# Two-part attention probabilities: one transposing transfer of 128 rows for each half tile in place of two of 64, and one planned time for every transposition

## The chip, the cores and the metric

One NeuronCore of a Trainium2 chip runs the whole program in one launch. The metric is device time in microseconds (us); several executions of a kernel are timed and their median is given. Engines are TensorE (PE, with its weight loads PEld), VectorE (DVE), ScalarE (ACT), GpSimd (POOL) and SyncE (SP), which here only issues transfers. Each engine works through its own instructions in the order in which the program lists them; semaphores order them across engines.

## The reference

```python
# q, k, v: (8 batches, 8 heads, 576 positions, 64), float32
scores = (1 / sqrt(64)) * q @ k.transpose(0, 1, 3, 2)
mask = (rel >= 0) & (rel < 64)            # rel = query position - key position
attn = softmax(where(mask, scores, -1e9))
x = (attn @ v).transpose(0, 2, 1, 3).reshape(8, 576, 512)
mixed = real(fft(fft(x, axis=1), axis=2))
u = x + mixed
un = (u - mean(u)) / sqrt(var(u) + 1e-06)     # over the last axis
out = u + maximum(un @ w_ch1, 0) @ w_ch2      # 512 -> 2048 -> 512
```

## The kernel before

The 8 x 576 rows of tokens are 36 tiles of 128 (`T` = 0 to 35, function `attn_tile`). Each pair of batches (nine tiles) then goes through a two-dimensional Fourier transform (`fft`), each tile through the normalization (`norm_tile`), and each pair of tiles is one *chunk* of 256 tokens of the feed-forward part (`ffn`, 18 chunks, 16 hidden blocks `f` each). In `ffn`, `ph` (L1213) is the first matrix product, `hh` its relu in two float16 parts (ACT L1228 writes the high part, DVE L1231 the low part), and `po` (L1194) the second product. The first chunk is computed in float32 (`PLAIN`), the others from float16 pairs, a high and a low part, in three passes (`PASSES`).

The attention of tiles 0 to 12 is in float32 (`whole`); its transpositions are done on PE. From tile 13 (`PRO`) on it is in two parts, and the transpositions are done by transfers that SP issues: `k_turn` (L493, into `kst`), two `q_turn` (L505, into `qbd`), and `p_turn` (L632, into `pt`). A tile has two half tiles (`jj` = 0, 1) of 64 queries and 8 heads. For one of them `score` (L581) leaves on each of 128 partitions (head parity x 64 queries) four head pairs x 128 keys; `masked` (L593, DVE) applies the mask and finds the maximum, `expo` (L601, ACT) the exponential, `p_hi` and `p_lo` (L403 and L413, or L407 where DVE does it) split it into the two parts in a buffer `flex[:, 1 + jj]`, seen as `pp` [128, 4, 2, 128] float16. `p_turn(0)` and `p_turn(1)` then transpose 64 rows of `pp` each into `pt` [128 keys, 2, 4, 2 x 64]. `av` (L663, PE) multiplies `pt` by the values `va`, `ve`, for both half tiles together, and `normed` (L671 to L675, DVE) divides by the sums. `y_turn` (L771, into `py`) and, in `norm_tile`, `u_turn` (L1056, into `uhl`, the input of a chunk) are transposing transfers too, of 128 rows x 1024 columns, as `k_turn` is.

The order of the instructions on every engine is made by a list scheduler, `Plan`, when the program is built. Each piece of work is an `op(engine, duration, priority, function, reads, writes, lat, alt)`. A transfer occupies the planner's engine "DMA" (SP's queue) for its duration, and what depends on it is thought ready `lat` later. `alt` names a second engine that may take the piece where it would be done sooner. `slack` adds half a microsecond before PE work that depends on a transfer (from tile 9 on). The numbers decide the order and the choice of engine only; on the chip semaphores decide. The lines of the transpositions before:

```python
TURN = 1.26
HTURN = 1.2
op("DMA", TURN, base + 0.2, k_turn, [bkp], [bkT], lat=2.0)
op("DMA", TURN, base + 0.7, lambda j=j: q_turn(j), Bfl[4:6], [Bq[i]], lat=2.8)
op("DMA", HTURN, base + 4.2 + jj, lambda g=p_turn: g(0), [bpp], [bt, bt2], lat=1.8)
op("DMA", HTURN, base + 4.3 + jj, lambda g=p_turn: g(1), [bpp], [bt2], lat=1.8)
op("DMA", TURN, base + 7.7, y_turn, [byp], [bpy], lat=2.2)
op("DMA", TURN, base + 0.95, u_turn, [bup, Bwl] if c >= 2 else [bup], [bu], lat=2.2)
```

The feed-forward products have the lowest priority (1e6 and up), so that PE takes them wherever no attention or Fourier work is ready.

Of the kernel before, what the change touches and what calls it, by code (L numbers as in the profile page):

```python
# [27 lines left out]
P = 128  # L28
# [8 lines left out]
NCH = NTT // 2  # L37
NKF = DFF // P
XR = 10
TURN = 1.26  # L40
HTURN = 1.2
Y_SOON = (4, 8)
LAZY, LAZY_FFT, LAZY_U = 0.2, 0.8, 0.5
LAZY_E, LAZY_Y = 0.3, 0.8
# [253 lines left out]
def attn_fft_ffn_kernel(ctx: ExitStack, tc: tile.TileContext, q, k, v, w1, w2, gidx, dft_d, dft_s, mask, out):  # L298
# [17 lines left out]
    def sb(shape, dt, tag, name):  # L316
        return pl.tile(shape, dt, tag=tag, name=name, bufs=RINGS[tag])
# [99 lines left out]
    def attn_tile(T, base):  # L417
# [145 lines left out]
        for jj in range(2):  # L563
# [61 lines left out]
                pp = t["pp", jj]  # L625
                both(eng, pp[:, :, 1], t["pr", jj], pp[:, :, 0], ALU.subtract)

            def p_turn(h, jj=jj):
                if h == 0:
                    t["pt", jj] = sb([P, 2, 4, P], F16, "pt", f"pt{T}_{jj}")  # L630
                dst = t["pt", jj][:, h].rearrange("p a (z s) -> p (a z) s", z=2)
                nc.sync.dma_start_transpose(dst, t["pp", jj][64 * h : 64 * h + 64].rearrange("p a z t -> p (a z t)"))  # L632

            op("ACT", 0.52, base + 4 + jj, p_hi, [bp], [bpp], alt=("DVE", 0.34, lazy))
            op("POOL", 1.12, base + 4.1 + jj, p_lo, [bp], [bpp], alt=("DVE", 0.6, lazy))
            bt2 = Buf()
            bpt[jj] = [bt, bt2]
            op("DMA", HTURN, base + 4.2 + jj, lambda g=p_turn: g(0), [bpp], [bt, bt2], lat=1.8)
            op("DMA", HTURN, base + 4.3 + jj, lambda g=p_turn: g(1), [bpp], [bt2], lat=1.8)

        bx, by = Buf("xu"), Buf("y")
        Bx[T] = bx
# [2 lines left out]
        for hf in range(2):  # L645
            bpa = Buf("ps")

            def av(hf=hf):
                if hf == 0:
                    xts[T] = sb([P, DM], F32, "xu", f"xu{T}")  # L650
                pa = t["pa", hf] = bank("ps", f"pa{T}_{hf}", (P, 4, 65))
                for hh in range(4):
                    h = 4 * hf + hh
                    if whole:
                        mm = [(slice(64 * (h % 2), 64 * (h % 2) + 64), None)]
                    else:
                        mm = [(slice(64 * a, 64 * a + 64), b_) for a, b_ in PASSES]

                    for x, (sl, b_) in enumerate(mm):
                        for jj, vt in enumerate(vts):  # L660
                            pt = t["pt", jj][:, h // 2] if whole else t["pt", jj][:, h % 2, h // 2]
                            v_ = vt[:, h] if whole else vt[:, b_, h]
                            nc.tensor.matmul(  # L663
                                pa[64 * jj : 64 * jj + 64, hh], pt[:, sl], v_, start=(x == 0), stop=(x == len(mm) - 1)
                            )
# [658 lines left out]
```

## Time and profile before

| what | value |
|---|---|
| median of 3 runs (lowest to highest) | 1008.24 us (1006.14 to 1009.97) |
| profiled execution | 1003.44 us, of it the span 1001.5 us |
| PE busy | 967.4 us (97%) |
| PE weight loads busy | 685.3 us (68%) |
| DVE busy | 665.6 us (66%) |
| ACT busy | 418.2 us (42%) |
| POOL busy | 260.9 us (26%) |
| chain that ended last, by engine | PE 80%, DMA 8%, SP 3%, DVE 3% |
| mean granted clock of TensorE | 0.996 |

The span runs from the first to the last instruction; the run's time is some 2 us longer. A profiled execution is one of many, here 4.8 us below the median of the timed ones.

### The profile page before, as it was taken

What the parts mean: (1) busy time and instruction counts of PE and PEld (TensorE: products, weight loads), DVE (VectorE), ACT (ScalarE), POOL (GpSimd) and SP (SyncE); (2) the same over time, 40 slices, a digit from 0 to 9 for tenths busy, and PEclk for the clock granted to TensorE, in tenths of its full rate; (3) what the DMA queues carried; (4) which work ended last, traced back from release to release, by engine and by line L of the source; (5) the groups of instructions that cost most, each with busy time, mean ns of one, the idle gap of its engine ahead of it and who ended that gap; (6) DMA issues with size and microseconds to landing.
All of it is one profiled execution on the core that took longest, in us unless ns stands there. A gap on an engine that the chain in (4) does not pass through costs nothing.

```text
span 1001.5 us, 22810 instructions
## 1 busy us (share of the span) xinstructions
PE 967.4 (97%) x8756; PEld 685.3 (68%) x8756; DVE 665.6 (66%) x1979; ACT 418.2 (42%) x1047; POOL 260.9 (26%) x537
## 2 busy tenths in 40 slices
PE   7889989999999989999999999999999999999998
PEld 6677757677776757676676667766676667666664
DVE  5899989888786768565796758676686745432121
ACT  6666656844554436323354426333454212121111
POOL 1000110136364623453032405343022400320000
PEclk9999999999999999999999999999999999999999
DMA  8987684225889877867768766968566311230000
GB/s 191 251 218 210 174 194 121 79 57 114 148 167 166 169 114 148 154 142 144 137 115 176 139 125 108 190 127 152 97 103 125 85 33 46 53 75 22 1 22 22
DMA packets 310540, 123.08 MB, mean 123 GB/s; under 512 B 292568, under 2 KB 292696, under 8 KB 310432
## 3 DMA queue, kind: packets, MB, share of 16 engines
q1 hardware_dynamic: 307712, 112.71, 55.4%
q0 software_dynamic: 2720, 8.92, 3.2%
q8 instruction: 69, 1.13, 0.5%
q14 instruction: 39, 0.32, 0.1%
HBM read 54.97 MB, written 14.17 MB: 69 GB/s over the span
## 4 chain that ended last, share of the span: by engine, by line
PE 80%; DMA 8%; SPq 3%; DVE 3%; issue 2%; ACT 2%; POOL 1%; DVEq 0%; POOLq 0%; ACTq 0%
PE ph L1213 34%; PE po L1194 32%; DMA kn<-in_k 3%; PE pa L663 3%; PE pz L930 2%; PE psc L581 2%; PE pg L896 2%; DMA pt<-flex 2%; PE psc L574 2%; POOL flex L413 1%; SPq L632 1%; DMA kst<-flex 1%; PE pp L612 1%; SPq L505 1%; DMA qn<-in_q 1%
## 5 line engine op out<-in xcount | busy, mean ns | idle before, releaser
L1213 PE MATMUL ph<-uhl,w0s 128*128 128x256 f16 (+1 forms) x3384 | 426.2, 277 | 4.3 <-DVE hh L1231 4.1
L1194 PE MATMUL po<-w1s,hh 128*128 128x512 f16 (+1 forms) x1696 | 426.0, 387 | 0.0
L1213 PEld LDWEIGHTS <-w0s 128*128 128x128 f16 x3264 | 317.7, 98 | 91.2 <-issue 8.0
L1231 DVE SCALAR_TENSOR_TENSOR hh<-ph,hh 128x256 f16<-128x256 f32 x272 | 114.5, 422 | 232.6 <-ACT hh L1228 228.9
L1228 ACT ACTIVATE hh<-ph 128x256 f16<-128x256 f32 x272 | 103.6, 382 | 382.2 <-PE ph L1213 288.2
L1194 PEld LDWEIGHTS <-hh 128*128 128x128 f16 x1632 | 156.5, 98 | 137.5
L601 ACT ACTIVATE pr<-pr,nm 128x128 f32<-128x128 f32 x288 | 90.9, 392 | 11.0 <-DVE nm L593 11.0
L593 DVE CUSTOM_DVE_ANT_0 pr<-psc,mskb 128x128 f32<-128x128 f32 x288 | 65.6, 284 | 15.7 <-PE psc L574 10.9
L413 POOL TENSOR_TENSOR up<-un,up 128x128 f16<-128x128 f32 x132 | 56.0, 452 | 64.8 <-ACT up L403 62.2
L413 POOL TENSOR_TENSOR flex<-kn,flex 128x128 f16<-128x128 f32 x76 | 40.4, 561 | 111.9 <-ACT flex L403 85.3
L413 POOL TENSOR_TENSOR flex<-pr,flex 128x128 f16<-128x128 f32 x92 | 38.7, 451 | 117.4 <-ACT flex L403 88.6
L1028 POOL TENSOR_TENSOR rs<-mv,mhalf 128x1 f32<-128x1 f32 x36 | 21.1, 585 | 139.9 <-DVE mv L1024 133.2
L1004 POOL DMA_INDIRECT mt<-md,gix x34 | 35.9, 1056 | 49.4 <-DMA md<-mp 42.8
L413 POOL TENSOR_TENSOR flex<-qn,flex 128x128 f16<-128x128 f32 x96 | 44.5, 496 | 14.1 <-ACT flex L403 10.9
L663 PE MATMUL pa<-va,pt 128*64 128x65 f16 (+1 forms) x760 | 38.9, 204 | 5.7 <-DMA pt<-flex 5.6
L663 PE MATMUL pa<-ve,pt 128*64 128x65 f16 (+1 forms) x760 | 39.3, 204 | 0.1
L403 ACT CAST flex<-pr 128x512 f16<-128x512 f32 x39 | 24.0, 615 | 24.1 <-DMA pt<-flex 22.9
L675 DVE TENSOR_TENSOR xu<-pa,rc 128x256 f32<-128x256 f32 x72 | 30.5, 424 | 2.6
L574 PE MATMUL psc<-kst,qbd 128*128 128x128 f32 x208 | 28.2, 282 | 3.5 <-ACT pt L403 1.5
L930 PE MATMUL pz<-g,ds__75 97*96 97x257 f16 (+3 forms) x240 | 29.2, 273 | 0.8 <-DVE g L906 0.8
L574 PEld LDWEIGHTS psc<-kst,qbd 128*128 128x128 f32 x208 | 25.1, 192 | 6.2 <-ACT pt L403 2.3
L663 PEld LDWEIGHTS <-pt 128*64 128x64 f16 x1104 | 20.3, 111 | 12.9 <-issue 6.6
(155 smaller groups left out, 1100.9 us busy)
## 6 DMA issues: line engine op xcount, KB each, us to landing
wd<-in_moe_w_ch SPq DMA_DIRECT2D x20, 512.0 KB, 4.7
out<-xu SPq DMA_DIRECT2D x36, 256.0 KB, 2.5
ve<-va SPq DMA_DIRECT2D x67, 130.0 KB, 3.3
kn<-in_k SPq DMA_DIRECT2D x32, 256.0 KB, 3.9
qn<-in_q SPq DMA_DIRECT2D x32, 256.0 KB, 4.7
flex<-in_moe_w_ch SPq DMA_DIRECT2D x12, 512.0 KB, 6.5
flex<-in_v SPq DMA_DIRECT2D x20, 256.0 KB, 3.5
md<-mp SPq DMA_DIRECT2D x24, 192.0 KB, 2.9
```

What stands on the lines that cost most here:

```text
L413: eng.tensor_tensor(out=out[:, k : k + w], in0=in0[:, k : k + w], in1=in1[:, k : k + w], op=al)
L574: nc.tensor.matmul(p_[:, hp], qw, keys(hp, jj), start=True, stop=True)
L593: nc.vector.tensor_tensor_reduce(out=t["pr", jj][:, hp], in0=t["ps", jj][:, hp], in1=mskb[:, m : m + P], scale=-0.125, scalar=3.0e38, op0= ...
L601: nc.scalar.activation(pr, pr, AF.Exp, bias=t["nm", jj][:, hp : hp + 1], scale=-1.0)
L663: nc.tensor.matmul(pa[64 * jj : 64 * jj + 64, hh], pt[:, sl], v_, start=(x == 0), stop=(x == len(mm) - 1))
L675: nc.vector.tensor_tensor(out=xv[:, 4 * hf : 4 * hf + 4], in0=pa[:, :, 0:64], in1=rc.to_broadcast([P, 4, 64]), op=ALU.mult)
L930: nc.tensor.matmul(pz[:M, c0:c1], ds_[:NJ, a, c[0] : c[0] + c[1]], t["g", gi][:, b_, c0:c1], start=(x == 0), stop=(x == len(mm) - 1),)
L1004: nc.gpsimd.indirect_dma_start(out=mts[T], out_offset=None, in_=mds[pb][0 : HR if n < 4 else 2 * HR], in_offset=bass.IndirectOffsetOnAxis( ...
L1194: nc.tensor.matmul(t["po"][i], l_, r_, start=(f == 0 and x == 0), stop=(f == NKF - 1 and x == len(mm) - 1))
L1213: nc.tensor.matmul(ph, l_, r_, start=(x == 0), stop=(x == len(mm) - 1))
L1228: nc.scalar.activation(t["hh", f][:, 0], ph, AF.Relu)
L1231: nc.vector.scalar_tensor_tensor(out=hh[:, 1], in0=ph, scalar=0.0, in1=hh[:, 0], op0=ALU.max, op1=ALU.subtract)
```

## The change

For each half tile of tiles 13 to 35 the two transfers of 64 rows become one of 128 rows, and `pt` is laid out as [128 keys, 4 pairs, 2 parts, 128 rows], from which `av` takes slices of 64 columns as before. The planner's time for this transfer and for the other transpositions (`k_turn`, `q_turn`, `y_turn`, `u_turn`) becomes 1.5, and the `lat` of `p_turn` 2.2. The transfers of k, q, y and u, the pieces into which the work is cut, and all arithmetic stay.

```diff
--- before.py
+++ after.py
@@ -37,8 +37,7 @@
 NCH = NTT // 2
 NKF = DFF // P
 XR = 10
-TURN = 1.26
-HTURN = 1.2
+TURN = 1.5
 Y_SOON = (4, 8)
 LAZY, LAZY_FFT, LAZY_U = 0.2, 0.8, 0.5
 LAZY_E, LAZY_Y = 0.3, 0.8
@@ -625,18 +624,14 @@
                 pp = t["pp", jj]
                 both(eng, pp[:, :, 1], t["pr", jj], pp[:, :, 0], ALU.subtract)
 
-            def p_turn(h, jj=jj):
-                if h == 0:
-                    t["pt", jj] = sb([P, 2, 4, P], F16, "pt", f"pt{T}_{jj}")
-                dst = t["pt", jj][:, h].rearrange("p a (z s) -> p (a z) s", z=2)
-                nc.sync.dma_start_transpose(dst, t["pp", jj][64 * h : 64 * h + 64].rearrange("p a z t -> p (a z t)"))
+            def p_turn(jj=jj):
+                t["pt", jj] = sb([P, 4, 2, P], F16, "pt", f"pt{T}_{jj}")
+                dst = t["pt", jj].rearrange("p a z s -> p (a z) s")
+                nc.sync.dma_start_transpose(dst, t["pp", jj].rearrange("p a z t -> p (a z t)"))
 
             op("ACT", 0.52, base + 4 + jj, p_hi, [bp], [bpp], alt=("DVE", 0.34, lazy))
             op("POOL", 1.12, base + 4.1 + jj, p_lo, [bp], [bpp], alt=("DVE", 0.6, lazy))
-            bt2 = Buf()
-            bpt[jj] = [bt, bt2]
-            op("DMA", HTURN, base + 4.2 + jj, lambda g=p_turn: g(0), [bpp], [bt, bt2], lat=1.8)
-            op("DMA", HTURN, base + 4.3 + jj, lambda g=p_turn: g(1), [bpp], [bt2], lat=1.8)
+            op("DMA", TURN, base + 4.2 + jj, p_turn, [bpp], [bt], lat=2.2)
 
         bx, by = Buf("xu"), Buf("y")
         Bx[T] = bx
@@ -651,14 +646,11 @@
                 pa = t["pa", hf] = bank("ps", f"pa{T}_{hf}", (P, 4, 65))
                 for hh in range(4):
                     h = 4 * hf + hh
-                    if whole:
-                        mm = [(slice(64 * (h % 2), 64 * (h % 2) + 64), None)]
-                    else:
-                        mm = [(slice(64 * a, 64 * a + 64), b_) for a, b_ in PASSES]
-
-                    for x, (sl, b_) in enumerate(mm):
+                    sl = slice(64 * (h % 2), 64 * (h % 2) + 64)
+                    mm = [(None, None)] if whole else PASSES
+                    for x, (a, b_) in enumerate(mm):
                         for jj, vt in enumerate(vts):
-                            pt = t["pt", jj][:, h // 2] if whole else t["pt", jj][:, h % 2, h // 2]
+                            pt = t["pt", jj][:, h // 2] if whole else t["pt", jj][:, h // 2, a]
                             v_ = vt[:, h] if whole else vt[:, b_, h]
                             nc.tensor.matmul(
                                 pa[64 * jj : 64 * jj + 64, hh], pt[:, sl], v_, start=(x == 0), stop=(x == len(mm) - 1)
```

As the planner's numbers change, the order changes on every engine from about 130 us of the program on. Line numbers of the changed kernel are 1 lower ahead of `p_turn` and 8 lower behind `av`. Three places follow; names with a number at their end are buffers.

SP's queue at tile 17 (`pt` of both half tiles, with the turns of k and q around them and a load of k), before:

```order
L632 DMA_TRANSPOSE pt_0_4881<-flex 128x8x64
L505 DMA_TRANSPOSE qbd_77<-flex 128x16x64
L493 DMA_TRANSPOSE kst<-flex 128x8x128
L632 DMA_TRANSPOSE pt_0_4881<-flex 128x8x64
L632 DMA_TRANSPOSE pt_1_4934<-flex 128x8x64
L505 DMA_TRANSPOSE qbd_77<-flex 128x16x64
L433 DMA kn_4964<-in_k 128x8x64
L632 DMA_TRANSPOSE pt_1_4934<-flex 128x8x64
```

The same place of the changed kernel:

```order
L630 DMA_TRANSPOSE pt_0_4882<-flex 128x8x128
L504 DMA_TRANSPOSE qbd_76<-flex 128x16x64
L432 DMA qn_4907<-in_q 128x8x64
L630 DMA_TRANSPOSE pt_1_4919<-flex 128x8x128
L504 DMA_TRANSPOSE qbd_76<-flex 128x16x64
L492 DMA_TRANSPOSE kst<-flex 128x8x128
L432 DMA kn_4987<-in_k 64x8x64 x2
```

The four issues into `pt` (8 x 64) have become two (8 x 128), one for each half tile, and a load of q stands between them.

DVE at the conversion of the last of the first matrix's weights (`wf_15`, three instructions, for which the first chunk's block 12, counted from 0, waits), behind the Fourier work of the second batch (`fs`, `h`), before:

```order
L413 TENSOR_TENSOR fs_1_1839<-f_1_1833,fs_1_1839 128x388
L413 TENSOR_TENSOR fs_1_1857<-f_1_1825,fs_1_1857 128x388
L1105 TENSOR_SCALAR wf_15_1864<-flex 128x512
L1110 SCALAR_TENSOR_TENSOR wf_15_1864<-flex,wf_15_1864 128x512
L1117 SCALAR_TENSOR_TENSOR wf_15_1864<-flex,wf_15_1864 128x512
L413 TENSOR_TENSOR h_1_1868<-yT_805 128x388
L413 TENSOR_TENSOR h_1_1877<-yT_805 128x388
```

The same place of the changed kernel:

```order
L412 TENSOR_TENSOR fs_1_1837<-f_1_1826,fs_1_1837 128x388
L412 TENSOR_TENSOR fs_1_1854<-f_1_1813,fs_1_1854 128x388
L412 TENSOR_TENSOR h_1_1862<-yT_805 128x388
L1097 TENSOR_SCALAR wf_15_1866<-flex 128x512
L1102 SCALAR_TENSOR_TENSOR wf_15_1866<-flex,wf_15_1866 128x512
L1109 SCALAR_TENSOR_TENSOR wf_15_1866<-flex,wf_15_1866 128x512
L412 TENSOR_TENSOR h_1_1872<-yT_805 128x388
```

One of the two additions into `h` has moved ahead of the three instructions on `wf_15`.

DVE between the statistics of tile 4 and those of tile 5 (these two tiles' normalized rows are the input of chunk 2); `un` is the scaled tile 4, `rc` and `xu` are `normed`, `w0s` and `w1s` are splits of weights. Before, behind the statistics of tile 4:

```order
L1231 SCALAR_TENSOR_TENSOR hh_10_2518<-ph_10_2490,hh_10_2518 128x256
L1231 SCALAR_TENSOR_TENSOR hh_11_2542<-ph_10_2490,hh_11_2542 128x256
L671 TENSOR_SCALAR rc_1_2547<-pa_1_2218 128x4
L674 RECIPROCAL rc_1_2547<-rc_1_2547 128x4
L675 TENSOR_TENSOR xu_2371<-pa_1_2218,rc_1_2547 128x256
L1170 SCALAR_TENSOR_TENSOR w1s<-w1s,s_89 128x512
L1032 TENSOR_SCALAR un_2571<-xu_651,mv_2515,rs_2540 128x512
L1231 SCALAR_TENSOR_TENSOR hh_12_2573<-ph_12_2551,hh_12_2573 128x256
L1170 SCALAR_TENSOR_TENSOR w1s<-w1s,s_89 128x512
```

The same place of the changed kernel:

```order
L1223 SCALAR_TENSOR_TENSOR hh_10_2597<-ph_10_2568,hh_10_2597 128x256
L663 TENSOR_SCALAR rc_0_2622<-pa_0_2543 128x4
L666 RECIPROCAL rc_0_2622<-rc_0_2622 128x4
L667 TENSOR_TENSOR xu_2542<-pa_0_2543,rc_0_2622 128x256
L663 TENSOR_SCALAR rc_1_2636<-pa_1_2554 128x4
L666 RECIPROCAL rc_1_2636<-rc_1_2636 128x4
L667 TENSOR_TENSOR xu_2542<-pa_1_2554,rc_1_2636 128x256
L1223 SCALAR_TENSOR_TENSOR hh_11_2634<-ph_10_2568,hh_11_2634 128x256
L1162 SCALAR_TENSOR_TENSOR w0s<-wf_15_1866,s_88,w0s 128x512
L1162 SCALAR_TENSOR_TENSOR w1s<-w1s,s_89 128x512
L1024 TENSOR_SCALAR un_2665<-xu_651,mv_2587,rs_2620 128x512
L1162 SCALAR_TENSOR_TENSOR w1s<-w1s,s_89 128x512
```

Before, one half of `normed` (tile 10) stood here; now two halves (tile 11) and a split into `w0s` stand here, and the scaling into `un` comes behind them. Of the rows not shown that stand ahead of tile 5's statistics, the changed kernel has two more half tiles' `masked` (tile 12), one more cast of weights on DVE (L404, which ACT did before) and one more split of weights (`w1s`); each of the two halves of `normed` of tile 11 came behind these statistics before, and that of tile 10 now stands ahead of tile 4's. On PE the changed kernel has three pieces ahead of chunk 2's first block that came behind it before: `flip_p` of tile 12 (L612), one half of `av` of tile 12 (L663) and `flip_y` of tile 11 (L756).

## Rows read from the trace of the kernel before

**Rows 1.** Busy time in two stretches of the span: the stretch, its length, busy us (and instructions) of PE, PEld, DVE, ACT and POOL, then the granted clock, the busy share of the DMA engines and GB/s.

```profile
200.00:250.00 50.00, 50.00 (x424) 35.04 (x423) 41.96 (x134) 22.83 (x54) 23.25 (x49) 1.00 0.39 86
250.00:800.00 550.00, 539.21 (x5432) 377.18 (x5431) 385.76 (x1164) 230.97 (x580) 199.67 (x412) 1.00 0.74 138
```

**Rows 2.** What PE waited for from 250 to 800 us: us in total, times, the longest.

```profile
PE pa L663 <- DMA pt<-flex: 5.6, 5, 2.1
PE ph L1213 <- DVE hh L1231: 4.1, 5, 1.3
PE py L756 <- DVE y L413: 0.8, 1, 0.8
```

**Rows 3.** PE's instructions behind these waits, in order of time: start, us, instruction, and in brackets PE's idle time before it and what ended it.

```profile
309.09 0.22 PE L663 MATMUL pa<-va,pt 128*64 128x65 f16 x1 [2.10 <-DMA pt<-flex]
362.30 0.22 PE L663 MATMUL pa<-va,pt 128*64 128x65 f16 x1 [1.43 <-DMA pt<-flex]
375.56 0.22 PE L663 MATMUL pa<-va,pt 128*64 128x65 f16 x1 [0.93 <-DMA pt<-flex]
412.54 0.22 PE L663 MATMUL pa<-va,pt 128*64 128x65 f16 x1 [0.73 <-DMA pt<-flex]
735.40 0.22 PE L663 MATMUL pa<-va,pt 128*64 128x65 f16 x1 [0.41 <-DMA pt<-flex]
459.29 0.27 PE L1213 MATMUL ph<-uhl,w0s 128*128 128x256 f16 x1 [1.30 <-DVE hh L1231]
545.37 0.27 PE L1213 MATMUL ph<-uhl,w0s 128*128 128x256 f16 x1 [1.25 <-DVE hh L1231]
```

**Rows 4.** The transposing transfers on SP: ns that the issue of one took (least, median, most) with the first and last start, and under each the us from issue to landing (least, median, most). L632 turns 64 rows, L1056 and L493 128 rows x 1024 columns, L505 64 rows x 2048 columns.

```profile
L632 SPq DMA_TRANSPOSE pt<-flex x92: 1192/1268/2390, 251.7 to 807.9; - x92
...
DMA to landing us min/median/max: 2.6/3.3/4.7
...
L1056 SPq DMA_TRANSPOSE uhl<-up x34: 1231/1241/2144, 122.5 to 893.3; - x34
...
DMA to landing us min/median/max: 3.0/3.4/5.4
...
L493 SPq DMA_TRANSPOSE kst<-flex x23: 1231/1314/3172, 157.0 to 723.9; - x23
...
DMA to landing us min/median/max: 3.3/3.8/4.3
...
L505 SPq DMA_TRANSPOSE qbd<-flex x46: 1242/1326/2503, 230.9 to 735.1; - x46
...
DMA to landing us min/median/max: 3.6/3.8/5.3
```

**Rows 5.** Pieces of the chain of work that ended last, around three of the waits: start, us, what.

```profile
302.03 7.01 DMA pt<-flex
...
309.09 0.85 PE pa L663 x41
...
452.09 4.92 DMA kst<-flex
...
537.70 5.28 DMA qbd<-flex
```

**Rows 6.** DVE, then PE, around the first chunk's wait for weights: start, us, instruction, idle time before it and what ended it.

```profile
144.48 0.43 DVE L1105 TENSOR_SCALAR w0s<-flex 128x512 int32<-128x512 int32 x1 [0.93 <-DMA flex<-in_moe_w_ch]
...
151.07 1.02 DVE L413 TENSOR_TENSOR h<-yT 128x388 f32<-128x388 f32 x2
...
151.23 0.80 PE L1213 MATMUL ph<-uhl,wf 128*128 128x256 f32 x1 [3.96 <-DVE wf L1117]
```

**Rows 7.** Three short stretches, columns as in Rows 1: just behind that wait, just behind the wait of 2.10 us, and DVE's stretch ahead of tile 5's statistics.

```profile
150.90:154.30 3.40, 3.07 (x7) 2.53 (x8) 3.33 (x8) 1.93 (x5) 0.00 (x0) 0.50 0.15 59
...
309.10:312.50 3.40, 3.40 (x60) 2.51 (x61) 2.12 (x8) 1.63 (x3) 1.95 (x5) 1.00 1.29 276
...
202.20:211.95 9.75, 9.75 (x68) 6.46 (x66) 8.03 (x26) 5.01 (x12) 3.20 (x6) 1.00 0.09 28
```

**Rows 8.** Around the start of chunk 2, in order of time on SP (the two turns of its input: start of the first, time to the end of the second), PE (a piece of the chain each for L663, two halves of `av`, and L756, then the timeline) and DVE (a cast; the first and the last of a half tile's four `masked`; a split; the first and the last instruction of two halves of `normed`).

```profile
211.18 7.61 SPq L1056 DMA_TRANSPOSE uhl<-up x2
...
214.84 1.08 PE pa L663 x32
...
221.34 0.44 PE py L756 x4
...
222.91 0.27 PE L1213 MATMUL ph<-uhl,w0s 128*128 128x256 f16 x1
...
195.21 0.49 DVE L405 TENSOR_SCALAR w1s<-w1s,s 128x512 f16<-128x512 f32 x1
...
209.63 0.28 DVE L593 CUSTOM_DVE_ANT_0 pr<-psc,mskb 128x128 f32<-128x128 f32 x1
...
210.26 0.28 DVE L593 CUSTOM_DVE_ANT_0 pr<-psc,mskb 128x128 f32<-128x128 f32 x1
...
211.29 0.74 DVE L1170 SCALAR_TENSOR_TENSOR w1s<-w1s,s 128x512 f16<-128x512 f32 x1
...
215.50 0.16 DVE L671 TENSOR_SCALAR rc<-pa 128x4 f32<-128x4 f32 x1 [0.28 <-PE pa L663]
...
216.65 0.42 DVE L675 TENSOR_TENSOR xu<-pa,rc 128x256 f32<-128x256 f32 x1
```

## The prediction

> **What bounds the kernel now.** I read the busy time by stretches first. From 200 to 250 us PE is never idle, and from 250 to 800 us, where all the two-part attention lies, it is idle for 550 - 539.2 = 10.8 us [rows 1]. So the products' own time sets the end, nothing that this change could do to transfers shortens them, and all that it can win in the stretch it acts on is 10.8 us, 1.1% of the span. The view of waits then says what those 10.8 us are: 5.6 us in five waits for turned probabilities, 4.1 us for relu parts, 0.8 us for a Fourier input [rows 2]. Five waits over 23 tiles: most turns land under feed-forward products and cost PE nothing. The timeline gives their sizes, 2.10, 1.43, 0.93, 0.73 and 0.41 us [rows 3]. The chain shows two more things. The longest wait ends a transfer that took 7.01 us from issue to landing, far over the median; and two of the waits for relu parts begin with other transposing transfers, one into `kst` of 4.92 us and one into `qbd` of 5.28 us [rows 5]: ACT's next piece waits for the buffer they read, and the relu behind it is late for PE.
>
> **The new transfer.** It removes 46 of 92 issues, 1.27 us of SP each [rows 4], some 58 us. SP computes nothing, so this counts only through landings. The trace has no 128-row turn of `pt`, but it has the same shape, 128 rows x 1024 columns, into `uhl` and `kst`: issue 1.24 to 1.31 us, landing 3.4 to 3.8 us after it [rows 4]. Twice the rows cost SP nothing more and the landing 0.1 to 0.5 us; I take 3.6. A pair of 64 rows issued back to back is complete 1.27 + 3.3 = 4.57 us after its first issue, the single one after 3.6: 0.97 us sooner. The planner takes part of this back. It thought the pair ready 1.2 + 1.2 + 1.8 = 4.2 us after the first issue and now thinks 1.5 + 2.2 = 3.7, so it puts `av` 0.5 us sooner into PE's queue. What PE wins at a wait is 0.97 - 0.5 = 0.47 us: 4 x 0.47 + 0.41 = 2.3 us. **Term: -2.3 us**, between 0 (the order is made anew, and the 7.01 us transfer was slow for another reason than its halves) and -5.6 (no wait left; with four issues in a row, 3 x 1.27 + 3.3 = 7.1 us become 1.27 + 3.6 = 4.9).
>
> The Trainium skill, "DMA: Bandwidth & Descriptors", section "Anatomy of one DMA — SWDGE (gpsimd) path", gives each transfer a fixed part of about 2.0 us beside its bytes. If every transfer saved gave that back, a wait would shrink by 2.0 - 0.5 = 1.5 us, an estimate from that page, the five by 5.0, and the sum below would be -3.0 instead of -0.3. The trace does not agree: a second issue starts 1.27 us behind the first while the first is in flight, so the fixed parts overlap.
>
> **The other transpositions.** Their code stays; the planner thinks them ready 0.24 us later (1.5 for 1.26). For k that is 3.50 us against 3.8 measured, for q 4.30 against 3.8 [rows 4]. Of the two relu waits behind such transfers, 1.30 and 1.25 us [rows 3, 5], that takes 2 x 0.24. **Term: -0.5 us**, between -2.55 (both gone) and 0; that new ones appear is a rival below.
>
> **The order ahead of tile 13.** Numbers that were nearly right are changed, and the order before the two-part tiles changes with them. Two places can be costed. At 151 us PE waits 3.96 us for the weights of the first chunk's block 12 (from 0). One addition of the Fourier work, half of 1.02 us, now stands ahead of their conversion on DVE instead of behind it [rows 6]. A cast moved from ACT to DVE some 20 us earlier ends ahead of DVE's own wait of 0.93 us for a load [rows 6] and is covered by it; without that cover it costs 0.49 [rows 8]. **Term: +0.5 us**, 0.5 to 1.0.
>
> The second place is the start of chunk 2. The two turns of its input end their issue at 218.8 us, so the second starts at 217.6; with 3.4 us to the landing [rows 4] the input is there at 221.0, and PE comes to it at 222.9 without idle time [rows 8]. The slack is 1.9 us. DVE now has more ahead of tile 5's statistics: two half tiles' masks (0.91 us each), two halves of `normed` (1.57), a cast (0.49) and a split (0.74): 4.6 us [rows 8]. PE has more too: two flips of 0.44 and half of 1.08, 1.4 us [rows 8]. What is left is 4.6 - 1.9 - 1.4 = 1.3 us of stall where there was none. If DVE's idle time ahead of it (9.75 - 8.03 = 1.7 us [rows 7]) is filled by the added work, nothing is left; if DVE waits once more as long, it is 3.0. An idle PE can also lose its clock: behind the idle 3.96 us the granted clock was 0.50 (1.2 GHz) for 3.4 us, behind 2.10 us it stayed at 1.00 (2.4 GHz) [rows 7]. At half the clock 3.4 us hold 1.7 us of work, so the worst is 3.0 + 1.7 = 4.7. I take 2.0, above the count, since the count leaves out every wait of DVE for ACT, and the added pieces wait for ACT or PE. **Term: +2.0 us**, 0 to 4.7.
>
> **Sum.** -2.3 - 0.5 + 0.5 + 2.0 = -0.3 us. On the profiled execution that is 1003.4 - 0.3 = 1003.1 us, a span of 1001.2. The profiled execution lies 4.8 us below the median of the runs, so the forecast for the median is 1008.24 - 0.3 = 1007.9 us. A measurement of this kernel can tell about 0.5%, 5.0 us, from no change; this is within.
>
> **Rivals.** *The waits go.* With SP relieved of 58 us all five waits on `pt` and both relu waits vanish, and chunk 2's input is in time: -5.6 - 2.55 + 0.5 = -7.7 us, 1000.6 us. For it: each of these waits is behind a transposing transfer [rows 3, 5]. Against it: the transfers into `kst` and `qbd` stay, and at 309 us the engines that move data are loaded beyond the normal (share 1.29 [rows 7]), which no order of issues changes.
>
> *ACT stands behind transfers oftener.* This ends on the other side. ACT's queue is in order; where a split of k, q or p waits for a landing, the relu behind it is late and PE waits 1.25 to 1.30 us, as at 459 and 545 us [rows 3]; landings of 4.92, 5.28 and 7.01 us [rows 5] against 3.5 to 4.3 planned show how. In the old order this befell two tiles of 23. The new order places 23 tiles anew; six more such places cost 6 x 1.25 = 7.5, and with the sum -0.3 + 7.5 = +7.2 us, 1015.4 us. It decides from five more places on (-0.3 + 6.25 = +6.0). For it: nothing in the planner knows that a landing can take 5 us. Against it: the planned times are now nearer to the measured ones.
>
> *The turn was hidden anyway.* Then the first term is 0 and the change is only a new order: -0.5 + 0.5 + 2.0 = +2.0 us, 1010.2 us. For it: 18 of the 23 tiles have no wait; against it: five have one [rows 3]. The Trainium skill, same page, section "Rules for kernel authors", speaks for this rival: a transfer issued early and waited for late has its fixed cost covered. The trace agrees with that rule wherever PE did not wait.
>
> **How the numbers follow.** The forecast has 0.53, the hidden turn 0.10, both within 5.0 us of before; the waits that go 0.15; ACT behind transfers 0.22. The likeliest case's own range runs from -5.6 - 0.5 + 0.5 + 0 = -5.6 to 0 + 0 + 1.0 + 4.7 = +5.7, so 1002.6 to 1013.9 us. For eight in ten I reach to the times of the two outer rivals, 1000.6 to 1015.4, which leaves out about half of each, 0.08 and 0.11. Chances: faster 0.15, within 0.63, slower 0.22.
>
> **What would show it.** SP issues 46 turns of `pt` of about 1.25 us with a median landing of 3.4 to 3.8 us. PE's waits for `pt` add up to 3.3 us and not 5.6; those for relu parts stay near 4. PE's wait at 151 us is about 4.5 us. Chunk 2's first `ph` stands behind 1 to 3 us of idle PE near 225 to 230 us. I am wrong if PE's idle time from 250 to 800 us leaves 4 to 14 us, or if the idle time at chunk 2 is over 5 us.

## Result, and the profile after

| what | before | after |
|---|---|---|
| median of the comparison (lowest to highest, runs) | 1008.08 us (1002.79 to 1013.28, 15) | 1013.29 us (1009.12 to 1021.94, 15) |
| profiled execution, of it the span | 1003.44 us, 1001.5 us | 1013.37 us, 1011.6 us |
| PE busy, PE idle in the span | 967.4 us, 34.1 us | 970.7 us, 40.9 us |
| DVE, ACT, POOL busy | 665.6, 418.2, 260.9 us | 672.9, 418.4, 265.4 us |

The changed kernel is slower: the ratio of after to before is 1.0056, 95% interval 1.0032 to 1.0079, some 5.6 us. The forecast was 1007.9 us and "within 0.5%"; the time came out 5.4 us above it, inside the range, in the direction that had a chance of 0.22. The two profiled executions lie 9.9 us apart, nearly twice the 5.2 us of the medians, because the one of before is 4.6 us below its median and the one of after at its own. So the traces are read for places and mechanisms, and prices are taken from the medians.

Busy time by stretches, with the columns of [rows 1], first of the kernel before and then of the changed kernel:

```profile
0.00:250.00 250.00, 230.56 (x1873) 173.47 (x1874) 212.51 (x662) 150.15 (x373) 41.79 (x87) 0.99 0.64 161
250.00:830.00 580.00, 569.21 (x5683) 397.88 (x5682) 401.29 (x1198) 237.14 (x594) 203.15 (x420) 1.00 0.71 133
```

```profile
0.00:250.00 250.00, 224.81 (x1818) 168.40 (x1819) 209.69 (x653) 149.60 (x372) 47.03 (x97) 0.99 0.66 162
250.00:830.00 580.00, 568.57 (x5668) 396.28 (x5666) 407.88 (x1205) 237.14 (x594) 202.11 (x390) 1.00 0.72 132
200.00:250.00 50.00, 45.69 (x389) 31.85 (x389) 40.67 (x114) 26.20 (x58) 21.46 (x45) 1.00 0.38 76
250.00:800.00 550.00, 538.57 (x5424) 376.20 (x5422) 390.76 (x1164) 229.58 (x576) 200.17 (x386) 1.00 0.74 137
```

PE's idle time (the stretch less PE's busy time) has grown from 250 - 230.56 = 19.4 to 25.2 us ahead of 250 us, and hardly in the stretch of the two-part attention, 10.8 to 11.4 us. That near equality hides an exchange. PE's waits from 250 to 800 us, which stand against [rows 2]:

```profile
PE ph L1205 <- DVE hh L1223: 11.4, 10, 4.0
```

One row is left. The five waits for turned probabilities, 5.6 us, are all gone, and those for relu parts have gone from 4.1 us in five to 11.4 us in ten. The transfer itself did what it was put in for; its issues on SP, as in [rows 4]:

```profile
L630 SPq DMA_TRANSPOSE pt<-flex x46: 1231/1276/2754, 256.9 to 812.1; - x46
...
DMA to landing us min/median/max: 3.1/3.1/6.9
```

Twice the rows take SP 1.28 us as before, and the median landing is 3.1 us, below the 3.3 us of 64 rows [rows 4]. The longest took 6.9 us, as the longest did before (7.01 us [rows 5]).

PE's instructions behind the larger new waits, in order of time (columns as in [rows 3]):

```profile
156.06 0.38 PE L1133 MATMUL pw<-few,unit 128*128 128x1 f32 x2 [1.01 <-DVE xu L667]
205.75 0.92 PE L1205 MATMUL ph<-uhl,w0s 128*128 128x256 f16 x7 [0.80 <-DVE hh L1223]
231.63 0.61 PE L1205 MATMUL ph<-uhl,w0s 128*128 128x256 f16 x4 [2.35 <-DMA uhl<-up]
327.39 0.81 PE L1205 MATMUL ph<-uhl,w0s 128*128 128x256 f16 x6 [4.02 <-DVE hh L1223]
482.14 0.59 PE L1205 MATMUL ph<-uhl,w0s 128*128 128x256 f16 x3 [2.38 <-DVE hh L1223]
```

The row at 231.63 us is the start of chunk 2, which waits 2.35 us for its input. The two turns of that input end their issue 11 us later than in [rows 8] (the pair of issues: start, time to the end of the second):

```profile
221.04 8.75 SPq L1048 DMA_TRANSPOSE uhl<-up  x2
```

The largest wait, 4.02 us, is worth following back. First DVE, then ACT, ahead of 327 us, each row with its engine's idle time and what ended it:

```profile
319.49 1.78 DVE L1011 TENSOR_TENSOR xu<-xu,mt 128x512 f32<-128x512 f32 x1 [1.25 <-DMA mt<-md,gix]
...
323.07 0.28 DVE L592 CUSTOM_DVE_ANT_0 pr<-psc,mskb 128x128 f32<-128x128 f32 x1
...
326.93 0.41 DVE L1223 SCALAR_TENSOR_TENSOR hh<-ph,hh 128x256 f16<-128x256 f32 x1
```

```profile
323.45 1.28 ACT L600 ACTIVATE pr<-pr,nm 128x128 f32<-128x128 f32 x4 [3.56 <-DVE nm L592]
324.68 0.62 ACT L402 CAST flex<-kn 128x512 f16<-128x512 f32 x1
325.21 0.38 ACT L1220 ACTIVATE hh<-ph 128x256 f16<-128x256 f32 x1
```

DVE stands for 1.25 us before an addition of the Fourier result, whose gather (`mt`) has not landed, and the addition then takes 1.78 us (0.69 us in the last experiment's rows below; why is open). The mask of a half tile is queued behind it, ACT's exponential waits 3.56 us for the maximum, and ACT's half of the relu stands behind the exponential. DVE's half is later still, behind more of its own queue, and PE has no `hh`. At 482 us it is a load of k that holds the same chain:

```profile
479.69 0.62 ACT L402 CAST flex<-kn 128x512 f16<-128x512 f32 x1 [2.76 <-DMA kn<-in_k]
480.22 0.62 ACT L402 ACTIVATE yp<-y 128x512 f16<-128x512 f32 x1
480.75 0.36 ACT L1220 ACTIVATE hh<-ph 128x256 f16<-128x256 f32 x1
```

Behind this wait the granted clock was at its lower level, 1.2 GHz, in a place where before it stayed at 2.4 GHz. At half the clock the 3.4 us of this stretch hold 1.7 us of work, so the wait cost 2.38 + 1.7, about 4 us:

```profile
482.40:485.80 3.40, 3.40 (x16) 1.90 (x14) 2.36 (x9) 1.11 (x4) 0.02 (x1) 0.50 0.83 160
```

### The profile page after: what moved, and what is told of

It reads as the page before. It is cut to its first block, busy times and chain, and to the rows that moved or that the text cites. A ratio compares the mean times of both kernels' runs of the same rounds, so it can differ in the third digit from the quotient of the medians.

```text
span 1011.6 us, 22762 instructions
## 1 busy us (share of the span) xinstructions
PE 970.7 (96%) x8756; PEld 685.5 (68%) x8756; DVE 672.9 (67%) x1985; ACT 418.4 (41%) x1048; POOL 265.4 (26%) x516
## 5 line engine op out<-in xcount | busy, mean ns | idle before, releaser
L1205 PEld LDWEIGHTS <-w0s 128*128 128x128 f16 x3264 | 318.0, 98 | 101.9 <-issue 17.1
L412 POOL TENSOR_TENSOR flex<-kn,flex 128x128 f16<-128x128 f32 x80 | 40.9, 541 | 117.2 <-ACT flex L402 115.6
L1020 POOL TENSOR_TENSOR rs<-mv,mhalf 128x1 f32<-128x1 f32 x36 | 23.8, 661 | 172.7 <-DVE mv L1016 171.7
L412 POOL TENSOR_TENSOR flex<-qn,flex 128x128 f16<-128x128 f32 x104 | 47.3, 490 | 19.3 <-ACT flex L402 18.3
L412 DVE TENSOR_TENSOR y<-xu 128x256 f32<-128x256 f32 x68 | 29.8, 479 | 0.7
```

The source lines that it names most:

```text
L412: eng.tensor_tensor(out=out[:, k : k + w], in0=in0[:, k : k + w], in1=in1[:, k : k + w], op=al)
L1205: nc.tensor.matmul(ph, l_, r_, start=(x == 0), stop=(x == len(mm) - 1))
```

## Experiments

The theory from these rows: the single transfer is a gain, and what is lost is lost to the order that the planner's new numbers make. The rival: the single transfer gains nothing, since its turn was hidden. A second question came up on the way: whether particular planned times carry the loss, or whether every remade order is a fresh draw. Ratios are to the kernel before on the same chip, with 95% intervals; idle time and waits are PE's, in us, from the stretches 0 to 250 and 250 to 830 us of one profiled execution (before: 19.4 and 10.8). For 1.27, 1.25, the later landings and both of the last two, that execution is the slowest of its kernel or within 0.1 us of it (1006.74, 1011.59, 1023.01 and 1013.67 us for medians of 1002.22, 1005.83, 1020.39 and 1010.19), so their idle times are high ones.

| run | ratio | idle to 250 | idle 250 to 830 | of it for relu parts | for landings directly |
|---|---|---|---|---|---|
| before | 1 | 19.4 | 10.8 | 4.1 | 5.6 |
| after | 1.0056 [1.0032, 1.0079] | 25.2 | 11.4 | 11.4 | 0 |
| times alone, pairs kept | 1.0154 [1.0128, 1.0179] | 25.0 | 15.4 | 7.1 | 8.0 |
| transfer's piece alone, others 1.26 | 1.0133 [1.0095, 1.0171] | 19.2 | 18.7 | 15.9 | 1.4 |
| old order, single transfers | 0.9941 [0.9918, 0.9963] | 19.6 | 8.1 | 7.4 | 0 |
| the same again | 0.9930 [0.9907, 0.9953] | 19.5 | 6.4 | 5.7 | 0 |
| new order, pairs | 1.0294 [1.0264, 1.0323] | 24.6 | 22.2 | 16.7 | 5.4 |
| old pieces, single transfers, 1.27 | 0.9968 [0.9947, 0.9989] | 19.1 | 10.4 | 8.1 | 2.2 |
| old pieces, single transfers, 1.25 | 0.9989 [0.9956, 1.0023] | 19.8 | 15.1 | 9.5 | 4.0 |
| transfer planned as the pair, others 1.26 | 0.9991 [0.9962, 1.0019] | 18.7 | 9.7 | 5.8 | 3.0 |
| after, landings planned 1 us later | 1.0145 [1.0101, 1.0189] | 23.1 | 17.1 | 5.4 | 11.5 |
| transfer planned as the pair, others 1.5 | 1.0069 [1.0038, 1.0100] | 23.2 | 6.1 | 5.1 | 0 |
| after, only `u_turn` 1.26 | 0.9993 [0.9966, 1.0019] | 20.3 | 12.2 | 8.0 | 3.6 |
| both of the last two | 1.0042 [1.0021, 1.0063] | 21.0 | 14.2 | 10.7 | 2.7 |

### The two halves of the change, one at a time

The kernel before with the planned times alone:

```diff
-TURN = 1.26
+TURN = 1.5
```

> Two transfers of 64 rows and their planned 1.2 us stay; only the planned time of the k, q, y and u transpositions becomes 1.5. If the loss comes from the new order that these numbers make, this is slower than before by 3 to 8 us and PE waits for relu parts more than 8 us from 250 to 800 us (before 4.1). If the loss comes from the single transfer or its own planned time, it is within 2 us of before. PE's waits for turned probabilities should stay near 5 us under both.

Measured: 1021.22 us against 1006.42, 1.0154, a larger loss than the 3 to 8 us expected. The same start as after (25.0 us of idle time to 250 us), and 3.6 us of waits for `pt` are still there, as the pairs are.

The changed kernel with only the transfer's own piece planned anew:

```diff
-TURN = 1.5
+TURN = 1.26
+PTURN = 1.5
...
-            op("DMA", TURN, base + 4.2 + jj, p_turn, [bpp], [bt], lat=2.2)
+            op("DMA", PTURN, base + 4.2 + jj, p_turn, [bpp], [bt], lat=2.2)
```

> One transfer of 128 rows with its planned 1.5 and 2.2 us; the planned time of the other transpositions stays 1.26. If the 1.5 for the others is what costs, this is at or below before (0 to -4 us), with no PE wait for turned probabilities. If any new order at this place costs, it is slower by 3 to 8 us, with more than 8 us of relu waits.

Measured: 1018.01 us, 1.0133, again more than the 3 to 8 us expected. Ahead of 250 us nothing is lost (19.2 us), behind it 15.9 us of waits for relu parts. Each half alone is slower than both together, so neither the times nor the transfer has a price of its own that could be added: each makes its own order.

### The transfer at an order that is held still

The kernel before, with the planner's two pieces for each half tile kept, so that the order on PE, DVE, ACT and POOL is the old one instruction for instruction. The first piece now issues the single transfer, the second nothing, so in SP's queue the transfer stands at the place of the first half (against the changed kernel):

```diff
-TURN = 1.5
+TURN = 1.26
+HTURN = 1.2
...
-            def p_turn(jj=jj):
+            def p_turn(h, jj=jj):
+                if h == 1:
+                    return
...
-            op("DMA", TURN, base + 4.2 + jj, p_turn, [bpp], [bt], lat=2.2)
+            bt2 = Buf()
+            bpt[jj] = [bt, bt2]
+            op("DMA", HTURN, base + 4.2 + jj, lambda g=p_turn: g(0), [bpp], [bt, bt2], lat=1.8)
+            op("DMA", HTURN, base + 4.3 + jj, lambda g=p_turn: g(1), [bpp], [bt2], lat=1.8)
```

> Every engine keeps the order of before; in SP's queue each pair of 64 rows is one transfer of 128 rows at the place of its first half. If the new order is the loss, this is faster than before: PE's 5.6 us of waits for turned probabilities fall to under 2 and nothing else moves, -3 to -6 us. If the single transfer itself costs (it lands later, or holds the movers longer), it is 0 to +5 us.

Measured: 1000.38 us against 1006.42, 0.9941, faster than both kernels. What PE waits for from 250 to 830 us:

```profile
PE ph L1211 <- DVE hh L1229: 7.4, 9, 2.2
PE py L754 <- DVE y L413: 0.7, 1, 0.7
```

No wait for `pt` is left. Something else moved, though the expectation said that nothing would: the waits for relu parts are 7.4 us, before they were 4.1. The opposite corner is the order of the changed kernel, held still, with two transfers of 64 rows issued back to back in place of each single one (against the kernel before):

```diff
-TURN = 1.26
-HTURN = 1.2
+TURN = 1.5
...
+            def p_turn(jj=jj):
+                t["pt", jj] = sb([P, 2, 4, P], F16, "pt", f"pt{T}_{jj}")
+                for h in range(2):
+                    dst = t["pt", jj][:, h].rearrange("p a (z s) -> p (a z) s", z=2)
+                    nc.sync.dma_start_transpose(dst, t["pp", jj][64 * h : 64 * h + 64].rearrange("p a z t -> p (a z t)"))
...
+            op("DMA", TURN, base + 4.2 + jj, p_turn, [bpp], [bt], lat=2.2)
```

> Every engine keeps the order of the changed kernel; each transfer of 128 rows is issued as two of 64 rows, back to back. If the new order is the loss, this is as slow as the changed kernel or slower, +5 to +10 us over before, with waits for turned probabilities added to the relu waits of 11 to 13 us. If the single transfer is the loss, it is back within 2 us of before.

Measured: 1034.98 us, 1.0294, and PE's waits from 250 to 830 us:

```profile
PE ph L1209 <- DVE hh L1227: 15.7, 14, 3.1
PE pa L659 <- DMA pt<-flex: 4.5, 5, 1.9
PE ph L1209 <- ACT hh L1224: 1.0, 1, 1.0
PE psc L580 <- DMA kst<-flex: 0.9, 1, 0.9
```

The four corners settle the first question. At one order the single transfer is worth -6 us (0.9941), at the other 22 to 24 us (1034.98 against 1013.29 us by the medians, 1.0294 against 1.0056 by the ratios). That the new order was planned for landings that a pair does not reach would explain the difference, and is not shown. The new order costs 1.0056 - 0.9941 = 1.2%, some 12 us, with single transfers and 2.9%, some 29 us, with pairs. The rival that the turn was hidden anyway is out.

The kernel of the old order with single transfers once more, unchanged, in another comparison:

> The kernel in the old order with one transfer for each pair once more, beside the kernel above on the same chip. If 0.994 was its own time and not that of one chip, the ratio is again 0.992 to 0.997, with no wait of PE for turned probabilities and 7 to 10 us of idle time from 250 to 830 us. If the first series was a lucky one, the ratio lies at 0.998 to 1.002.

Measured: 998.66 us against 1006.28, 0.9930, again without a wait for `pt`.

### How much an order changes for nothing

The kernel of the old order with single transfers, planned with 1.27 and with 1.25 in place of 1.26; a hundredth of a microsecond says nothing about the chip:

```diff
-TURN = 1.26
+TURN = 1.27
```

> As the old order with single transfers (1000.4 us there), but planned with 1.27 for the other transpositions in place of 1.26, a hundredth of a microsecond, which remakes the order. If the order of before is merely a lucky one among many, this loses 5 to 13 us against that kernel (1005 to 1013 us) through other relu waits. If the loss of the changed kernel comes from what 1.5 and 3.7 us say (times too short for the single turn, too long for the others), a hundredth does nothing: 998 to 1003 us.

```diff
-TURN = 1.26
+TURN = 1.25
```

> The same with 1.25, a hundredth below. Lucky order: 1005 to 1013 us, not the same waits as with 1.27. Planned times as the cause: 998 to 1003 us.

Measured: 1002.22 us (0.9968) and 1005.83 us (0.9989), against 0.9941 and 0.9930. The first lies in the band expected for planned times as the cause, the second in that for a lucky order, so the two do not decide between them. They do show that a step without meaning moves this kernel by some 0.3 to 0.6%, as much as the whole effect of the change (0.6%). The sizes are rough: the interval of 1.25 (0.9956 to 1.0023) lies above that of the second series at 1.26 (0.9907 to 0.9953) and overlaps that of the first, and 1.27 overlaps both.

### Is it the planned length of the transfer?

The kernel with the transfer's piece alone, but planned as the pair was, 2.4 us of queue and ready 1.8 us later:

```diff
-PTURN = 1.5
+PTURN = 2.4
...
-            op("DMA", PTURN, base + 4.2 + jj, p_turn, [bpp], [bt], lat=2.2)
+            op("DMA", PTURN, base + 4.2 + jj, p_turn, [bpp], [bt], lat=1.8)
```

> One transfer of 128 rows, planned as one piece that takes as long as the two halves did (2.4 of the queue, ready 1.8 later, 4.2 us in all); the other transpositions planned at 1.26. If a plan that thinks the turn slower than it is protects ACT's queue, 998 to 1004 us and relu waits from 250 to 800 us under 8. If any remade order loses, 1008 to 1020 us as with the planned 1.5 and 2.2 (1018.0).

Measured: 1005.43 us, 0.9991, some 12.6 us less than with 1.5 and 2.2, and between the two times expected; the relu waits, 5.8 us, are under the 8 expected of a plan that protects ACT's queue. A planned time that is longer than the measured one gave the better order.

Then the changed kernel with every transposition thought ready 1 us later, durations as they were (`lat` 2.0, 2.8 and 2.2 become 3.0, 3.8 and 3.2; one of the five lines is shown):

```diff
...
-            op("DMA", TURN, base + 4.2 + jj, p_turn, [bpp], [bt], lat=2.2)
+            op("DMA", TURN, base + 4.2 + jj, p_turn, [bpp], [bt], lat=3.2)
...
```

> The changed kernel with every transposition planned to land 1.0 us later; durations stay at 1.5. If its relu waits come from landings that are later than planned, they fall from 11.4 to under 6 us and the time to 1003 to 1008 us. If they come from the order as such, the time stays within 1010 to 1020 us.

Measured: 1020.39 us, 1.0145. Waits for relu parts fell to 5.4 us, but 11.5 us of direct waits for landings (`pt` 6.5, `uhl` 5.0) took their place. More caution in the planner is no cure.

### Two prices, alone and together

From the runs so far one could read two separate losses. All kernels with 1.5 for `u_turn` have 3.7 to 5.8 us more idle time ahead of 250 us than the kernel before, and none with 1.26 has more than 0.4; and the kernels with a short time for the transfer lose most behind it. Three runs test that. The changed kernel with the transfer planned as the pair:

```diff
+PTURN = 2.4
...
-            op("DMA", TURN, base + 4.2 + jj, p_turn, [bpp], [bt], lat=2.2)
+            op("DMA", PTURN, base + 4.2 + jj, p_turn, [bpp], [bt], lat=1.8)
```

> The single transfer with all other transpositions planned at 1.5 us, as in the change, but the transfer itself planned to occupy the queue 2.4 us and to be ready 1.8 us later (the price that the pair had), the value that took 12.6 us from the kernel with 1.26 us elsewhere. Theory A (two separate losses: the 1.5 us of the turns of k, q, y and u costs the start of the feed-forward part, before 250 us; the short queue time of the probabilities' turn costs the stretch from 250 to 830 us): PE's idle time to 250 us stays at about 25 us, that from 250 to 830 us stays near 10 us, and the time is 1005 to 1011 us, ratio 0.998 to 1.004. Theory B (every remade order is a draw of its own, and the planned numbers say nothing): idle time from 250 to 830 us anywhere from 8 to 22 us, the middle of the draws so far 15 us, time about 1015 us. Theory C (the 1.5 us is the whole cost, early and late, as with the old pairs): idle time from 250 to 830 us at 15 us, time 1018 to 1022 us.

Measured: 1010.47 us against 1004.70, 1.0069. The idle time behaved as two separate losses would have it, 23.2 and 6.1 us, the least late idle time of all. The time did not follow: 1010.47 us is within the 1005 to 1011 us of that theory, but on a chip whose kernel before is faster, and the ratio is above its 0.998 to 1.004. In the profiled execution PE is busy for 975.2 us, 4.4 us more than in the changed kernel, since the lower clock was granted for longer (mean granted clock 0.990 against 0.995). That is not the reason for the median: three other executions of this kernel with a mean clock of 0.996 or 0.997 took 1009.22 to 1010.49 us. Why the median is not lower is open. One of the stretches at the lower clock, behind chunk 2's wait of 2.37 us (columns as in [rows 7]):

```profile
234.60:238.00 3.40, 3.40 (x29) 2.54 (x28) 3.07 (x10) 0.38 (x1) 1.61 (x4) 0.50 0.70 104
```

The changed kernel with `u_turn` alone at 1.26:

```diff
+UTURN = 1.26
...
-            op("DMA", TURN, base + 0.95, u_turn, [bup, Bwl] if c >= 2 else [bup], [bu], lat=2.2)
+            op("DMA", UTURN, base + 0.95, u_turn, [bup, Bwl] if c >= 2 else [bup], [bu], lat=2.2)
```

> The changed kernel with only the turn of the feed-forward input (u_turn) planned at 1.26 us again; those of k, q, p and y stay at 1.5. It is the only transposition planned ahead of tile 13, so the order up to about 200 us is that of the kernel before. Theory A (two separate losses): PE's idle time to 250 us falls from 25.2 to 19 to 20 us and the stall of 2.35 us at the start of chunk 2 is gone; from 250 to 830 us it stays above 11 us, since the short queue time of the probabilities' turn stays; time 1008 to 1014 us. Theory B (a draw of its own): idle time to 250 us unforeseeable between 19 and 25 us, that from 250 to 830 us between 8 and 22 us.

Measured: 1004.86 us, 0.9993, 0.6% less than the changed kernel and below the 1008 to 1014 us of the theory of two losses. The idle time to 250 us is 20.3 us, the later one 12.2 us, both as that theory had them, and the issues of chunk 2's input stand where they stood before (210.73 us against 221.04):

```profile
210.73 7.62 SPq L1049 DMA_TRANSPOSE uhl<-up  x2
```

Both repairs together, against the changed kernel:

```diff
+PTURN = 2.4
+UTURN = 1.26
...
-            op("DMA", TURN, base + 4.2 + jj, p_turn, [bpp], [bt], lat=2.2)
+            op("DMA", PTURN, base + 4.2 + jj, p_turn, [bpp], [bt], lat=1.8)
...
-            op("DMA", TURN, base + 0.95, u_turn, [bup, Bwl] if c >= 2 else [bup], [bu], lat=2.2)
+            op("DMA", UTURN, base + 0.95, u_turn, [bup, Bwl] if c >= 2 else [bup], [bu], lat=2.2)
```

> Both repairs together: the turn of the feed-forward input planned at 1.26 us, the single transfer of the probabilities planned at 2.4 us of queue and 1.8 us to the landing, and the turns of k, q and y at 1.5 us. Theory A (two separate losses that add): PE's idle time to 250 us is 19 to 20 us, as in the kernel with the turn of the input alone at 1.26, and that from 250 to 830 us is 5 to 9 us, as in the kernel with the pair's price; the time is that of the old order with single transfers, ratio 0.993 to 0.998. Theory B (every remade order is a draw of its own): idle time to 250 us still 19 to 20 us, since that order is not remade, but from 250 to 830 us the middle of the draws, 12 to 13 us (8 to 19), ratio 0.999 to 1.004.

Measured: 1010.19 us against 1006.28, 1.0042. Here the theory of two losses that add falls. The early one stayed repaired (21.0 us, no stall of chunk 2), the late one did not, by the ratio (0.993 to 0.998 expected) and in the profiled execution, the slowest of twelve, by the idle time: 14.2 us where 5 to 9 were expected. The largest part of it, 5.35 us, is one place; PE's instruction, DVE's queue ahead of it, and the clock behind it:

```profile
314.17 0.58 PE L1207 MATMUL ph<-uhl,w0s 128*128 128x256 f16 x2 [5.35 <-DVE hh L1225]
```

```profile
305.37 0.42 DVE L1225 SCALAR_TENSOR_TENSOR hh<-ph,hh 128x256 f16<-128x256 f32 x1
311.96 0.69 DVE L1013 TENSOR_TENSOR xu<-xu,mt 128x512 f32<-128x512 f32 x1 [6.17 <-DMA mt<-md,gix]
...
313.70 0.41 DVE L1225 SCALAR_TENSOR_TENSOR hh<-ph,hh 128x256 f16<-128x256 f32 x1
```

```profile
314.20:317.60 3.40, 3.40 (x40) 2.33 (x41) 0.81 (x2) 0.68 (x2) 3.07 (x6) 0.50 0.30 85
```

DVE waited 6.17 us for a gather with a relu part queued four instructions behind it. What is shown: the early loss belongs to `u_turn`'s planned time (23.1 to 25.2 us of idle time to 250 us with 1.5, 18.7 to 21.0 with 1.26). What the late loss follows is not any one number that was tried: with single transfers and remade orders the ratios spread from 0.9968 to 1.0145, and none of the nine reached the old order's 0.993 to 0.994. Why the old order is the better one is open; that it was a good draw among many would fit, and is not shown.

## Why the prediction was wrong, point by point

**What bounds the kernel.** Right. PE is busy for 96% of the span, and what changed hands was PE's idle time.

**The new transfer, -2.3 us.** The mechanism was right, the size too small: at the old order the medians fall by 6.0 and 7.6 us, beyond the lower bound of -5.6 us. The landing is 3.1 us (after) to 3.5 us (the old order with single transfers), where 3.6 was taken. The larger error is "issued back to back". In the kernel before the second issue of a half tile starts 2.48 us behind the first in the median of the 46 (1.24 to 6.12 us, over 2 us in 30), not 1.27, since other transfers stand between, as at tile 17 in the rows of the change. SP ahead of the wait of 2.10 us (start, time to the end of the last of a row's issues):

```profile
295.83 1.30 SPq L632 DMA_TRANSPOSE pt<-flex  x1
...
298.19 2.51 SPq L632 DMA_TRANSPOSE pt<-flex  x2
...
302.03 1.37 SPq L632 DMA_TRANSPOSE pt<-flex  x1
```

The second half of the later half tile is issued last, at 302.03 us, and it is the one that landed 7.01 us later [rows 5]. By these medians a single transfer in the first half's place is there 2.48 + 3.3 - 3.5 = 2.3 us sooner, an estimate, where 0.97 was counted. How much of the 6.0 us belongs to the one transfer and how much to the place in the queue is not separated: no run issued the halves back to back at the old order. Nor do the traces show all of it: the waits for `pt` are gone, but with the relu waits PE's idle time from 250 to 830 us falls only from 10.8 to 8.1 and 6.4 us, and the profiled execution of before (1003.44 us) is a fast one. The gain was docked by 0.5 us a wait for a planner that comes sooner; with the order held still that docking is not there, and with the order made anew it is not the measure of what the order does. The 2.0 us that the prediction tried as another price stand in the Trainium skill, "DMA: Bandwidth & Descriptors", section "Anatomy of one DMA — SWDGE (gpsimd) path", for transfers that GpSimd issues; the turns here are issued by SP. The Trainium skill, "DMA: Bandwidth & Descriptors", section "Rules for kernel authors", advises one transfer of 128 partitions in place of two to disjoint halves, since the two share the same engines. The trace agrees with the advice: a pair of 64 rows, even back to back, was complete 1.27 + 3.3 = 4.57 us after its first issue by the medians, the single one after 3.1 to 3.5, and at the same order one for two is worth 0.6 to 0.7%. That shared engines are the reason no run here shows.

**The other transpositions, -0.5 us.** Wrong in sign. This term took two waits for relu parts behind turns of k and q and made them 0.24 us shorter. Those two are gone, and ten others came: from 4.1 to 11.4 us (7.1 with the new times alone). Planned times closer to the measured ones did not make a better order; the times alone cost 1.5%.

**The order ahead of tile 13, +0.5 and +2.0 us.** At 151 us PE waits 4.08 us for 3.96, so the first is +0.1. The start of chunk 2 waits 2.35 us, as forecast, though by larger terms than mine: the turns of its input end at 229.9 us for 218.8, 11.1 us later where 4.6 were counted, and PE comes there at 231.63 - 2.35 = 229.3 us for 222.9, 6.4 us later where 1.4 were counted. DVE shows what the first count lacked: it comes to tile 5's statistics at 222.35 us for 212.67, 9.7 us later, and from 150 us to there it is busy 60.82 us for 56.20, just the 4.6 us counted, but idle for 5.1 us more. That the two delays left nearly the stall that was taken is in part luck. The failed step is the sentence "Two places can be costed", from which the sum went on as if there were two. PE has seven other new waits between 155 and 250 us, 0.28 to 1.01 us each and 3.7 us together (the largest at 156.06 and 205.75 us). They are most of what lies between the 2.5 us forecast and the 25.2 - 19.4 = 5.8 us found there.

**The sum, -0.3 us.** Its failed step is the one that prices a remade order by the places that can be read beforehand. In 23 two-part tiles it named two relu waits and let them improve. The runs show some +12 us for the new order with single transfers, where the sum has 0.5 + 2.0 - 0.5 = +2.0 us and the half microsecond a wait inside its first term. With the -6 us of the transfer that makes the measured +0.56%. The lower end of the likeliest case's range also takes -0.5 for the other transpositions, whose own bound was -2.55; with that it would be the first rival's -7.7 us. The measured time lies at the upper end.

**The rivals.** *ACT stands behind transfers oftener* named the direction and the size, +7.5 us of relu waits where the trace has +7.3, and the form, an engine in order with the relu behind something that has not landed. The transfers are others than those named: of the 11.4 us, 4.0 lie behind a gather on DVE, 3.2 behind loads of k and 2.0 behind turns of the feed-forward input. Five small waits are left, 2.1 us together; a turn of q is part of one, as ACT stands 0.32 us for it ahead of the wait of 0.99 us at 423.50 us. As it counted on other places, that its size came true is in part luck. It would have given 1015.4 us. *The waits go* was right on the waits for `pt` and wrong that nothing takes their place. *The turn was hidden anyway* is refuted by the four corners.

**What would show it.** The issues (46, 1.28 us) are as said, the landing is 0.3 us below the least value given. The waits for `pt` are 0, not 3.3 us; those for relu parts 11.4, not about 4. PE's wait at 151 us is 4.08 us where 4.5 was said, and chunk 2's 2.35 us are within the 1 to 3. The bounds set for being wrong, idle time from 250 to 800 us outside 4 to 14 us and over 5 us at chunk 2, were not crossed (550 - 538.57 = 11.4 us, and 2.35): a sum over a stretch can stay while all that it is made of changes.

## What to carry to other kernels

Where a scheduler's table is changed together with an operation, hold the order still and change the operation alone first; here that gave 0.993 to 0.994, while the same operation with its "right" numbers gave 1.0056. A remade order on engines that work in order is a term of its own, and its size can be had cheaply by moving a number by a hundredth: here 0.3 to 0.6%, as large as the edit's own effect. Read which loads, gathers and turns stand ahead of the work that the busiest engine waits for, not only those that the change names.

## What the runs showed of the hardware that was not expected

**A crowded place that none of these orders avoids.** Around 305 us the engines that move data are busier than on average (0.68 to 0.73 from 250 to 830 us): their busy share from 305 to 310 us is 1.40 before, 1.26 after, 1.10 and 1.53 in the two runs of the old order with single transfers, 1.31 with both repairs, and least, 0.75, with the transfer's piece alone. The crowd moves with the order: in each of the fourteen profiled executions one of the four slices of 5 us from 300 to 320 us has 1.10 to 1.55. So the prediction's "which no order of issues changes" holds roughly for the place, and not for the size. Something is late there, though not always the same: 7.01 us for a turn of `pt` before [rows 5], 6.9 us for one after, and for the gathers of `mt` between 285 and 330 us up to 5.3 us before, 6.9 after and 8.4 with both repairs. The last of these, with DVE's wait:

```profile
  DMA mt<-md,gix: 6.2, 1
...
DMA to landing us min/median/max: 3.6/4.6/8.4
```

PE loses between nothing (`u_turn` alone at 1.26, busy without a break from 290 to 330 us) and 5.35 us there. That the crowding makes them late is argued from the two standing together; no run took the load away.

**The clock does not follow from the length of a wait alone.** The lower level was granted behind waits of 2.37, 2.38 and 5.35 us (the rows above), and the higher one stayed behind waits of 2.35 and 4.02 us. The changed kernel behind these two:

```profile
231.70:235.10 3.40, 2.92 (x37) 2.45 (x38) 3.13 (x11) 0.39 (x1) 2.82 (x7) 1.00 0.59 137
327.40:330.80 3.40, 3.40 (x26) 2.48 (x26) 3.34 (x14) 1.54 (x5) 0.00 (x0) 1.00 0.76 82
```

**The same kernel's profiled execution can lie far from its median.** With 1.25 the single runs go from 999.46 to 1011.62 us, and the profiled one took 1011.59. A wait of 4 us in one trace is not a price of 4 us.
